# Reordered engine queues inside an attention slot, earlier operand splits, a third raw weight buffer and a ring of six accumulator banks

## The chip, the cores and the metric

One core of a Trainium2 chip runs the whole program. The metric is device time in microseconds (us), median of several runs. The engines of the core each work through a queue of their own in order: PE (matmul), ACT (activations and copies), DVE (vector work), POOL (a second, slower vector engine), and SP, which here only starts DMAs. They wait for each other through semaphores.

## The reference, cut to what matters

Causal attention by blocks of 64 over 4 batches, 8 heads and 576 positions of 64 values, followed by two feed-forward layers of 512 to 2048 to 512 over the 2304 tokens.

```python
def _attn_ref(q, k, v):
    scores = scale * np.matmul(q, k.transpose(0, 1, 3, 2))
    mask = block_i >= block_j
    scores = np.where(mask, scores, -1000000000.0)
    scores = scores - np.max(scores, axis=-1, keepdims=True)
    attn = np.exp(scores)
    attn = attn / (np.sum(attn, axis=-1, keepdims=True) + 1e-09)
    return np.matmul(attn, v)

def _moe_ref(x, w_in, w_out, alpha):
    h = x @ w_in
    g = np.maximum(h, 0.0) + alpha * np.minimum(h, 0.0)
    return g @ w_out

def _moe2_ref(x, w_in, w_out):
    h = x @ w_in
    g = np.where(h > 0.0, h, np.exp(np.minimum(h, 0.0)) - 1.0)
    return g @ w_out
```

The weights arrive as 64-bit floats; the kernel turns each into two 32-bit parts itself.

## The kernel before, in words

**Three passes for one product.** Every operand of a matmul is split into a high and a low part (`fp32r`), and a product is three matmuls: high by high, high by low, low by high (`PASSES`). So q, k, x, the gates and the weights all need a "high" copy and then a "low" one, which is the value less its high part. `copy("p", ...)` (line 88) puts a high part on POOL, `low_part` (line 81) a low part on DVE or POOL, `q_low` (line 226) the low part of q on DVE.

**Attention in slots.** `SEQ` lists 64 slots. The first 16, called early here, take one pair of heads each over the first 256 positions. The other 48, called late, go three to a pair of heads: i = 2 and i = 3 take 128 queries each, i = 4 the last 64 of both heads. `slot(k)` (line 459) writes one slot into the queues, and the order of its lines is the order on every engine: `scores` (PE), the product with v of an older slot (`second`, PE), the transposes of a slot two or three back (PE), then the sums and reciprocals of the slot before (`normalise`, DVE, and the scaling of p on POOL, line 88), then `maxima` (memsets of the mask and the maxima, DVE), the gates that wait in `held`, the copies of the finished x (`out`, ACT then DVE), the copies of the transposes (`move`, ACT and DVE), then `exponentials` (ACT, line 321), and at the end whatever was planned for the slot in `other_at`. Scores go to one of two PSUM pairs in turn, transposes to banks 4 and 5, x to banks 6 and 7.

**Splits and loads.** `load_early` and `load_late` start the DMAs of the raw q and k, `split_early_k`, `split_early_q`, `split_k` and `split_late_q` make the parts. Early slots share one split for two slots (a duo d, used in slots 2d and 2d+1). The plan is in lines 441 to 453: k of a duo at the end of slot 2d-2, q at the end of slot 2d-1; in the late part k three slots ahead and q two slots ahead of the first use.

**Weights.** `load_w` (line 110) starts one DMA of 512 KB into a buffer `wraw` (pool of two), and plans five steps for the following ticks: two on ACT, three on DVE (lines 130, 131, 135), one on POOL (line 140), a cast on ACT and the low part on DVE.

**The first layer beside the attention.** `l1_beside` puts the matmuls of the first layer for three token units between the slots from slot 11 on (lines 527 and 550).

**After the attention** only the order on PE is written by hand. Steps go over token units (five of 512, 512, 512, 512 and 256) and blocks of 128 hidden values: `l1_h` or `l2_h` makes one bank of h (lines 527, 571), and two steps later `l1_y` or `l2_y` adds its product into four accumulator banks (lines 614, 589). h goes round a ring of four banks, the accumulators are banks 2 to 5 for every unit (`ACC`). At a unit's end the accumulators are copied out (`to_z`, line 531, or line 621).

Of the kernel before, what the change touches and what calls it, by code (L numbers as in the profile page):

```python
# [19 lines left out]
P = 128  # L20
# [21 lines left out]
def attention_moe_kernel(ctx: ExitStack, tc: tile.TileContext, qT, kT, v_a, v_b, w1, w2, alpha, out):  # L42
# [6 lines left out]
    wraw_p = ctx.enter_context(pool("wraw", 2))  # L49
# [7 lines left out]
    nc.sync.dma_start(out=alpha_sb, in_=alpha)  # L57

    beta = const.tile([P, NF], F32, name="beta")
    dve.tensor_scalar(beta, alpha_sb, -1.0, 1.0, ALU.mult, ALU.add)  # L60
# [134 lines left out]
    def load_early(d):  # L195
        b, hs = duo(d)
        st[2 * d]["raw"] = raws = raw_tiles()
        for t, src in zip(raws[::-1], (kT, qT)):
            for a in range(2):
                h = slice(hs.start + 2 * a, hs.start + 2 * a + 2)  # L200
                nc.sync.dma_start(out=t[:, 256 * a:256 * a + 256],
                                  in_=src[b, h].rearrange("e p s -> (e p) s")[:, :256])
# [33 lines left out]
    def split_q(n, c):  # L236
        s = st[n]
        q = s["raw"][0]
        s["q"] = tiles = [ap2.tile([P, 512], F32R, tag=f"q{x}", name=f"q{x}") for x in "hl"]
        qh, ql = (t[:, :c.stop - c.start] for t in tiles)  # L240
        copy("a" if c.start == 0 and n == 0 else "p", qh, q[:, c], 0.125)
        q_low(ql, q[:, c], qh)
# [5 lines left out]
    def split_early_q(d):  # L248
        split_q(2 * d, slice(0, 512))
        st[2 * d + 1]["q"] = st[2 * d]["q"]  # L250

    def split_late_q(n):
        s = st[n]
        split_q(n, slice(256, 512))
        s["diag"] = dh, dl = qdiag[n % 2]
        q = s["raw"][0]
        for x in range(2):
            r, c = slice(64 * x, 64 * x + 64), slice(64 * x, 64 * x + 64)
            copy("p", dh[r, c], q[r, 512:], 0.125)
            q_low(dl[r, c], q[r, 512:], dh[r, c])  # L260
# [121 lines left out]
    def parts_of_x(n, half):  # L382
# [3 lines left out]
        if half == 1:  # L386
            tail = st[n]["tail"] = ap1.tile([P, 2, 64], F32R, tag="xtail", name="xtail")
            parts.append((slice(256, 320), lambda k: tail[:, k, :]))
# [12 lines left out]
    def second(n, half, chunks):  # L401
# [39 lines left out]
    for d in range(NP // 2):  # L441
        if d:
            plan(2 * d - 2, lambda d=d: split_early_k(d))
            plan(2 * d - 1, lambda d=d: split_early_q(d))
        if d > 1:
            plan(2 * d - 3, lambda d=d: load_early(d))
            plan(2 * d, lambda d=d: load_early_v(d))
    for n in range(NP):
        k = NP + 3 * n
        plan(k - 5, lambda n=n: load_late(n))  # L450
        plan(k - 3, lambda n=n: split_k(n, S))
        plan(k - 2, lambda n=n: split_late_q(n))
        plan(k + 2, lambda n=n: load_late_v(n))
    NORM = transposes_at.pop("norm")
# [4 lines left out]
    def slot(k):  # L459
# [15 lines left out]
        if here:  # L475
            exponentials(*here)
# [107 lines left out]

    def l2_y(u, f, gs):
        for tg in range(UNITS[u] // P):
            acc = bank[ACC[tg]]
# [17 lines left out]
    def l1_y(kind, u, f, gs):  # L605
# [5 lines left out]
        for m in range(KC):  # L611
            acc = bank[ACC[m]][:, :n]
# [14 lines left out]
    ACC = (2, 3, 4, 5)  # L627
    ET = mybir.EngineType
    with tc.manual_schedule(engines={ET.PE, ET.Activation, ET.DVE, ET.Pool, ET.SP}):
# [43 lines left out]
    with tc.manual_schedule(engines={ET.PE}):  # L673
# [7 lines left out]
        ring("h", 6, 7, 0, 1)  # L681
# [66 lines left out]
```

## Time and profile before

| what | value |
|---|---|
| median of 3 runs | 1078.89 us (1077.31 to 1943.81) |
| the profiled execution, its own time | 1077.87 us |
| span of the profiled execution | 1076.1 us |
| instructions | 13977 |
| mean granted clock of PE | 0.974 |
| PE busy | 989.7 us |

A row of the trace gives start and duration in us, engine, line, operation, and in brackets how long the engine was idle before it and what ended that. "PEclk" is the share of the full PE clock that was granted: 1.00 is 2.4 GHz, 0.50 is 1.2 GHz, and a value between them is a mix over the stretch.

### The profile page before, as it was taken

The numbers are of one execution on the slowest core, as the hardware profiler recorded it, in microseconds if no ns is written. First come the engines' busy times: TensorE is split into PE (matmuls) and PEld (weight loads), VectorE is DVE, ScalarE is ACT, GpSimd is POOL, SyncE is SP. The second block draws the span as 40 slices with busy tenths as digits, with TensorE's granted clock in tenths as the row PEclk, the third lists the DMA queues.
The fourth block names the chain that finished last, engine by engine and source line by source line (L and its number), as shares of the span: only waits on it lengthen the run. The fifth ranks groups of instructions, "written<-read, shape, count | busy, mean of one in ns | idle before, by whom it ended". The sixth has DMA issues, their size and how long they took to land.

```text
span 1076.1 us, 13977 instructions
## 1 busy us (share of the span) xinstructions
PE 989.7 (92%) x5072; PEld 789.9 (73%) x5072; DVE 560.8 (52%) x1067; ACT 440.5 (41%) x965; POOL 349.8 (33%) x410
## 2 busy tenths in 40 slices
PE   4667998988888999999999998899999999999998
PEld 3445765655557987788888886688888888888897
DVE  4677576776745787631131577873333333333343
ACT  4556565655544655432232455542222222222222
POOL 4665566765623555442232455420000000000000
PEclk9888998999899999999999999899999999999999
DMA  4461622452355655350230635510300300110010
GB/s 119 138 211 38 202 88 78 135 169 83 115 164 186 191 168 182 110 160 36 79 118 1 210 123 177 193 42 1 118 1 1 118 1 1 40 40 1 1 40 20
DMA packets 54437, 104.73 MB, mean 97 GB/s; under 512 B 10976, under 2 KB 28384, under 8 KB 53216
## 3 DMA queue, kind: packets, MB, share of 16 engines
q1 hardware_dynamic: 54368, 103.84, 29.7%
q8 instruction: 40, 0.66, 0.2%
q14 instruction: 29, 0.24, 0.1%
HBM read 75.51 MB, written 28.31 MB: 96 GB/s over the span
## 4 chain that ended last, share of the span: by engine, by line
PE 53%; DVE 15%; POOL 11%; DMA 7%; issue 6%; ACT 6%; SPq 1%; POOLq 0%; ACTq 0%
PE bank L589 17%; PE bank L571 16%; PE bank L614 7%; PE bank L527 7%; DMA wraw<-w 6%; POOL wword L140 3%; POOL p L88 3%; DVE wword L130 2%; DVE wword L135 2%; DVE wword L131 2%; ACT p L321 2%; DVE stat L293 2%; PE bank L550 2%; DVE w L81 2%; POOL gs L81 2%
## 5 line engine op out<-in xcount | busy, mean ns | idle before, releaser
L527 PE MATMUL bank<-x,w 128*128 128x512 f32 (+1 forms) x960 | 214.1, 372 | 3.6 <-DVE xtail L81 1.5
L571 PE MATMUL bank<-x,w 128*128 128x512 f32 (+1 forms) x960 | 211.2, 369 | 0.0
L527 PEld LDWEIGHTS bank<-x,w 128*128 128x128 f32 x960 | 169.2, 191 | 34.5 <-issue 1.6
L571 PEld LDWEIGHTS bank<-x,w 128*128 128x128 f32 x960 | 170.3, 189 | 31.6
L576 DVE TENSOR_SCALAR e<-e 128x512 f32<-128x512 f32 (+1 forms) x80 | 33.1, 414 | 169.2 <-ACT e L575 169.2
L575 ACT ACTIVATE e<-bank 128x512 f32<-128x512 f32 (+1 forms) x80 | 44.4, 555 | 181.8 <-PE bank L571 181.8
L140 POOL TENSOR_TENSOR wword<-wword,wraw 128x512 int32<-128x512 int32 x64 | 89.6, 1402 | 82.0 <-DVE wword L135 44.0
L589 PE MATMUL bank<-w,gsl 128*128 128x512 f32 x432 | 107.2, 395 | 3.8 <-DVE z L621 2.6
L510 DVE SCALAR_TENSOR_TENSOR g<-neg,beta,bank 128x512 f32<-128x512 f32 (+1 forms) x68 | 46.3, 681 | 116.1 <-ACT neg L507 116.1
L88 POOL TENSOR_SCALAR p<-p,stat 128x128 f32<-128x128 f32 (+4 forms) x144 | 79.7, 568 | 78.8 <-DVE stat L327 45.5
L589 PE MATMUL bank<-w,gs 128*128 128x512 f32 x432 | 104.9, 390 | 0.2 <-DVE gs L81 0.2
L614 PE MATMUL bank<-gsl,w 128*128 128x512 f32 (+1 forms) x408 | 90.9, 369 | 7.5 <-POOL gsl L81 3.0
L589 PEld LDWEIGHTS bank<-w,gsl 128*128 128x128 f32 x432 | 81.1, 190 | 22.1 <-ACT e L575 3.0
L81 POOL TENSOR_TENSOR gs<-g,gs 128x512 fp32r<-128x512 f32 (+1 forms) x46 | 57.7, 1254 | 111.9 <-ACT gs L514 103.6
L614 PE MATMUL bank<-gs,w 128*128 128x512 f32 (+1 forms) x408 | 89.5, 366 | 4.5 <-POOL gs L81 4.4
L589 PEld LDWEIGHTS bank<-w,gs 128*128 128x128 f32 x432 | 80.5, 188 | 17.0 <-DVE gs L81 0.7
L321 ACT ACTIVATE p<-pair,stat 128x128 f32<-128x128 f32 (+4 forms) x144 | 78.3, 552 | 34.9 <-DVE stat L293 32.9
L614 PEld LDWEIGHTS bank<-gsl,w 128*128 128x128 f32 x408 | 71.2, 191 | 22.1 <-POOL gsl L81 5.0
L614 PEld LDWEIGHTS bank<-gs,w 128*128 128x128 f32 x408 | 70.4, 189 | 18.8 <-POOL gs L81 6.1
L81 DVE TENSOR_TENSOR w<-wword,w 128x512 fp32r<-128x512 f32 x64 | 59.6, 934 | 25.0 <-ACT w L149 24.0
L507 ACT ACTIVATE neg<-bank 128x512 f32<-128x512 f32 (+1 forms) x68 | 36.9, 542 | 87.2 <-PE bank L527 87.1
L81 POOL TENSOR_TENSOR gsl<-g,gsl 128x512 fp32r<-128x512 f32 (+1 forms) x34 | 42.2, 1242 | 76.7 <-ACT gsl L514 71.9
(77 smaller groups left out, 1310.3 us busy)
## 6 DMA issues: line engine op xcount, KB each, us to landing
wraw<-w SPq DMA_DIRECT2D x64, 512.0 KB, 3.6
xd<-x SPq DMA_DIRECT2D x4, 2048.0 KB, 7.2
x<-xd SPq DMA_DIRECT2D x16, 512.0 KB, 7.7
x<-yd SPq DMA_DIRECT2D x4, 2048.0 KB, 8.6
vraw<-v_a SPq DMA_DIRECT2D x24, 256.0 KB, 2.9
kraw<-kT SPq DMA_DIRECT2D x16, 288.0 KB, 4.0
yd<-gsl SPq DMA_DIRECT2D x8, 512.0 KB, 4.7
yd<-gs SPq DMA_DIRECT2D x8, 512.0 KB, 6.2
```

Source lines behind the costliest of these rows:

```text
L81: return {"v": dve, "p": pool_e}[eng].tensor_tensor(out=out, in0=x, in1=f32(high), op=ALU.subtract)
L88: return pool_e.tensor_scalar(out, x, 1.0 if scale is None else scale, 1.0, ALU.mult, ALU.mult)
L140: pool_e.tensor_tensor(out=w, in0=w, in1=units, op=ALU.add)
L321: act.activation(out=out, in_=x, func=AF.Exp, bias=stat[:, k:k + 1], accum_out=stat[:, w + k:w + k + 1])
L507: act.activation(out=neg, in_=h, func=AF.Relu, scale=-1.0)
L510: dve.scalar_tensor_tensor(out=g, in0=neg, scalar=beta[:, f:f + 1], in1=h, op0=ALU.mult, op1=ALU.add)
L527: pe.matmul(h, w_in(0, f, wp_, kc), x[:, xp_, kc, :n], start=kc == 0 and t == 0, stop=kc == KC - 1 and t == 2)
L571: pe.matmul(h, w_in(1, f, wp_, kc), x[:, xp_, kc, :], start=kc == 0 and t == 0, stop=kc == KC - 1 and t == 2)
L575: act.activation(out=e, in_=h, func=AF.Exp)
L576: dve.tensor_scalar(e, e, 1.0, -1.0, ALU.min, ALU.add)
L589: pe.matmul(acc, gs[:, gp_, tg * P:(tg + 1) * P], w_out(1, f, wp_, 0, DM), start=f == 0 and t == 0, stop=f == NF - 1 and t == 2)
L614: pe.matmul(acc, w_out(0, f, wp_, m * P, P), gs[:, gp_, :n], start=first and t == 0, stop=last and t == 2)
```

## The change

1. In `slot`, `maxima` goes ahead of the sums (`NORM`), and `exponentials` directly behind them, ahead of the copies of x and of the transposes.
2. The splits come sooner. In the early part the high part of q and both parts of k at the end of slot 2d-3, the low part of q a slot later; in the late part the high parts of q move to three slots ahead, in front of k, and the low parts stay at two. Loads are started one to three slots sooner. The first loads are ordered anew, and the first q comes through ACT's queue.
3. `alpha` is loaded after the first weights; `beta` is first written by an ACT copy.
4. In `out` both ACT copies come ahead of both DVE low parts, and `xtail` has two buffers.
5. `wraw` and `wword` have three buffers; the tiles for gates outside `gp` go from four, used every second time, to two, used every third time.
6. After the attention h has a ring of two banks (6 and 7), and the accumulators go round a ring of six (0 to 5).

```diff
-    wraw_p = ctx.enter_context(pool("wraw", 2))
+    wraw_p = ctx.enter_context(pool("wraw", 3))
...
-    nc.sync.dma_start(out=alpha_sb, in_=alpha)
-
     beta = const.tile([P, NF], F32, name="beta")
-    dve.tensor_scalar(beta, alpha_sb, -1.0, 1.0, ALU.mult, ALU.add)
+    act.copy(beta, ident[:, :NF])
+
+    def load_alpha():
+        nc.sync.dma_start(out=alpha_sb, in_=alpha)
+        dve.tensor_scalar(beta, alpha_sb, -1.0, 1.0, ALU.mult, ALU.add)
...
-        for t, src in zip(raws[::-1], (kT, qT)):
+        for t, src, eng in zip(raws[::-1], (kT, qT), (nc.sync, nc.sync if d else nc.scalar)):
...
-    def split_q(n, c):
+    def split_q(n, c, low):
...
+        if low:
+            q_low(ql, q[:, c], qh)
+        else:
+            copy("a" if c.start == 0 and n == 0 else "p", qh, q[:, c], 0.125)
...
-            tail = st[n]["tail"] = ap1.tile([P, 2, 64], F32R, tag="xtail", name="xtail")
+            tail = st[n]["tail"] = ap2.tile([P, 2, 64], F32R, tag="xtail", name="xtail")
...
-                for c, dst in parts_of_x(n, half):
+                parts = parts_of_x(n, half)
+                for c, dst in parts:
                     act.copy(dst(0), op[:, c])
+                for c, dst in parts:
                     low_part("v", dst(1), op[:, c], dst(0))
...
-    for d in range(NP // 2):
-        if d:
-            plan(2 * d - 2, lambda d=d: split_early_k(d))
-            plan(2 * d - 1, lambda d=d: split_early_q(d))
+    for d in range(1, NP // 2):
+        plan(2 * d - 3, lambda d=d: split_early_q(d, False))
+        plan(2 * d - 3, lambda d=d: split_early_k(d))
+        plan(2 * d - 2, lambda d=d: split_early_q(d, True))
         if d > 1:
-            plan(2 * d - 3, lambda d=d: load_early(d))
+            plan(2 * d - 6, lambda d=d: load_early(d))
...
-        plan(k - 5, lambda n=n: load_late(n))
+        plan(k - 6, lambda n=n: load_late(n))
+        plan(k - 3, lambda n=n: split_late_q(n, False))
         plan(k - 3, lambda n=n: split_k(n, S))
-        plan(k - 2, lambda n=n: split_late_q(n))
+        plan(k - 2, lambda n=n: split_late_q(n, True))
...
+        if here:
+            maxima(*here)
         for emit in NORM.get(k, ()):
             emit()
         if here:
-            maxima(*here)
+            exponentials(*here)
         after = [h() for h in held]
         held.clear()
         for o in outs:
             o()
         if move:
             move()
-        if here:
-            exponentials(*here)
...
-        if late_pools and turn[0] % 2:
-            return late_pools[0].tile([P, 2, 512], F32R, tag="gsl", name="gsl", bufs=4)
+        if late_pools and turn[0] % 3 == 0:
+            return late_pools[0].tile([P, 2, 512], F32R, tag="gsl", name="gsl", bufs=2)
...
-            acc = bank[ACC[tg]]
+            acc = acc_bank(tg, f == 0)
...
-            acc = bank[ACC[m]][:, :n]
+            acc = acc_bank(m, first)[:, :n]
...
         load_early(0)
-        load_w(*halves.pop(0))
+        load_early(1)
+        split_early_q(0, False)
+        split_early_k(0)
+        split_early_q(0, True)
         load_early_v(0)
         load_w(*halves.pop(0))
-        load_early(1)
+        load_alpha()
+        for emit in other_at[-1]:
+            emit()
         load_early_v(1)
-        split_early_k(0)
-        split_early_q(0)
+        load_w(*halves.pop(0))
...
-        ring("h", 6, 7, 0, 1)
+        ring("h", 6, 7)
+        ring("acc", *range(6))
```

**DVE, two early slots.** The rows are those of DVE in slots 5 and 6, first as they stood. `stat` holds maxima, sums and reciprocals of a slot, `pair` its scores, `x` the finished attention output, `pt` the transposed p, `wword` a weight half in work.

```order
L326 TENSOR_SCALAR stat<-stat 128x4
L327 RECIPROCAL stat<-stat 128x4
L296 MEMSET pair_103 64x2x64 x2
L293 TENSOR_REDUCE stat<-pair_103 128x2 x2
L81 TENSOR_TENSOR x_310<-bank_106,x_310 128x256
L87 COPY pt<-bank_104 128x2x128
L226 SCALAR_TENSOR_TENSOR ql<-qraw,qh 128x512
L130 TENSOR_SCALAR wword<-wword 128x512
```

The same place on DVE in the changed kernel:

```order
L302 MEMSET pair_102 64x2x64 x2
L299 TENSOR_REDUCE stat<-pair_102 128x2 x2
L332 TENSOR_SCALAR stat<-stat 128x4
L333 RECIPROCAL stat<-stat 128x4
L83 TENSOR_TENSOR x_332<-bank_105,x_332 128x256
L89 COPY pt<-bank_103 128x2x128
L132 TENSOR_SCALAR wword<-wword 128x512
L133 TENSOR_SCALAR wword<-wword 128x512
L137 SCALAR_TENSOR_TENSOR wword<-wraw,wword 128x512
```

The maxima stand ahead of the sums of the slot before, and the low part of q has left this slot for the even one.

**ACT, an early slot.** The rows of ACT over slots 5 and 6 as they stood; `p` is the exponentials.

```order
L418 CAST x_310<-bank_106 128x256
L85 COPY pt<-bank_105 128x2x256
L321 ACTIVATE p_426,stat<-pair_103,stat 128x128 x2
L321 ACTIVATE p_426,stat<-pair_103,stat 128x256 x2
L418 CAST x_310<-bank_107 128x256
```

The same place on ACT in the changed kernel:

```order
L327 ACTIVATE p_439,stat<-pair_102,stat 128x128 x2
L327 ACTIVATE p_439,stat<-pair_102,stat 128x256 x2
L425 CAST x_332<-bank_105 128x256
L87 COPY pt<-bank_104 128x2x256
L327 ACTIVATE p_492,stat<-pair_101,stat 128x128 x2
```

The high part of x, on which DVE's low part of x waits, has gone from ahead of the slot's exponentials to behind them.

**POOL, a late pair of heads.** The rows of POOL as they stood, from the scaling of an i = 4 slot on; `gs` is a gate of the first layer, `kh` and `kl` the parts of k, `qh` and `qdiag` those of q.

```order
L88 TENSOR_SCALAR p_1607<-p_1607,stat 128x576
L81 TENSOR_TENSOR gs<-g,gs 128x512
L88 TENSOR_SCALAR kh<-kraw 128x576
L81 TENSOR_TENSOR kl<-kraw,kh 128x576
L88 TENSOR_SCALAR p_1654<-p_1654,stat 128x384 x2
L88 TENSOR_SCALAR qh<-qraw 128x256
L88 TENSOR_SCALAR qdiag_118<-qraw 64x64 x2
```

The same place on POOL in the changed kernel:

```order
L90 TENSOR_SCALAR p_1600<-p_1600,stat 128x576
L83 TENSOR_TENSOR gs<-g,gs 128x512
L90 TENSOR_SCALAR qh<-qraw 128x256
L90 TENSOR_SCALAR qdiag_117<-qraw 64x64 x2
L90 TENSOR_SCALAR kh<-kraw 128x576
L83 TENSOR_TENSOR kl<-kraw,kh 128x576
L90 TENSOR_SCALAR p_1652<-p_1652,stat 128x384 x2
```

The high parts of q have moved ahead of k and of the next scaling; their low parts on DVE stay where they were, one slot later.

## Rows read from the trace of the kernel before

**Rows 1.** The page, part 1: busy us, share of span, instructions per engine.
```profile
PE 989.7 (92%) x5072; PEld 789.9 (73%) x5072; DVE 560.8 (52%) x1067; ACT 440.5 (41%) x965; POOL 349.8 (33%) x410
```

**Rows 2.** Windows: stretch, length, busy per engine, then PEclk, DMA share, GB/s.
```profile
8.40:67.20 58.80, 39.21 (x264) 28.56 (x264) 39.84 (x107) 34.34 (x121) 36.94 (x62) 0.91 0.41 130
67.20:105.90 38.70, 26.29 (x167) 19.65 (x166) 28.22 (x62) 22.13 (x68) 21.23 (x35) 0.82 0.34 113
105.90:296.60 190.70, 170.76 (x1055) 116.15 (x1054) 132.85 (x331) 110.55 (x280) 120.31 (x172) 0.95 0.40 124
320.40:460.00 139.60, 130.04 (x731) 112.85 (x732) 94.97 (x137) 73.17 (x142) 69.27 (x57) 0.99 0.53 169
600.00:720.00 120.00, 112.19 (x473) 89.63 (x472) 97.43 (x138) 65.28 (x113) 54.21 (x37) 0.97 0.44 149
720.00:1020.00 300.00, 300.00 (x1325) 248.50 (x1324) 104.31 (x174) 70.88 (x117) 0.00 (x0) 1.00 0.08 29
```

**Rows 3.** Waits, whole program: waiter, what ended it, total us, times, longest.
```profile
ACT e L575 <- PE bank L571: 181.8, 71, 3.0
...
DVE ql L226 <- POOL qh L88: 34.2, 18, 4.3
ACT xtail L418 <- DVE x L81: 34.0, 14, 5.1
...
PE pair L276 <- POOL qh L88: 23.4, 6, 5.5
```

**Rows 4.** Timeline of the start, ACT and PE.
```profile
6.33 1.28 ACT L85 ACT_TABLE_LOAD   x1 [6.33 <-DMA qraw<-qT]
...
8.40 0.47 PE L276 MATMUL pair<-kh,qh 64*128 64x128 f32 x2 [8.40 <-ACT qh L85]
```

**Rows 5.** Timeline of one early slot from its maxima on, DVE and ACT.
```profile
46.81 0.42 DVE L296 MEMSET pair<- 64x128 f32 x2
...
48.20 0.41 DVE L81 TENSOR_TENSOR x<-bank,x 128x256 fp32r<-128x256 f32 x1
48.32 0.37 ACT L321 ACTIVATE p<-pair,stat 128x128 f32<-128x128 f32 x1 [0.70 <-DVE stat L293]
48.53 0.41 DVE L87 COPY pt<-bank 128x256 f32<-128x256 f32 x1
...
49.20 0.69 DVE L226 SCALAR_TENSOR_TENSOR ql<-qraw,qh 128x512 fp32r<-128x512 f32 x1 [0.26 <-POOL qh L88]
49.81 0.42 DVE L130 TENSOR_SCALAR wword<-wword 128x512 f32<-128x512 f32 x1
49.92 0.63 ACT L149 CAST w<-wword 128x512 fp32r<-128x512 f32 x1
...
51.34 0.16 DVE L326 TENSOR_SCALAR stat<-stat 128x4 f32<-128x4 f32 x1
...
51.73 0.42 DVE L296 MEMSET pair<- 64x128 f32 x2
```

**Rows 6.** Timeline, DVE: where the maxima of slots 4, 11 and 16 begin.
```profile
31.20 0.42 DVE L296 MEMSET pair<- 64x128 f32 x2 [1.09 <-PE pair L276]
...
69.32 0.42 DVE L296 MEMSET pair<- 64x128 f32 x2
...
106.80 0.17 DVE L301 MEMSET pair<- 64x128 f32 x1 [0.54 <-PE pair L276]
```

**Rows 7.** Late part: one timeline row of DVE, one wait of window 105.9:296.6.
```profile
254.68 0.44 DVE L226 SCALAR_TENSOR_TENSOR ql<-qraw,qh 128x256 fp32r<-128x256 f32 x1 [4.35 <-POOL qh L88]
...
PE bank L356 <- ACT pt L85: 12.7, 8, 2.5
```

**Rows 8.** Timeline, PE: first matmul into an accumulator bank at two unit changes.
```profile
349.63 0.63 PE L614 MATMUL bank<-gsl,w 128*128 128x256 f32 x3 [2.88 <-ACT z L85]
...
680.08 0.94 PE L589 MATMUL bank<-w,gsl 128*128 128x512 f32 x3 [2.57 <-DVE z L621]
```

**Rows 9.** Timeline, DVE and POOL: a low part of q beside POOL's addition.
```profile
74.96 1.27 POOL L140 TENSOR_TENSOR wword<-wword,wraw 128x512 int32<-128x512 int32 x1
75.03 1.75 DVE L226 SCALAR_TENSOR_TENSOR ql<-qraw,qh 128x512 fp32r<-128x512 f32 x1 [2.73 <-POOL qh L88]
```

More of the change, by code (lines that the diff above doesn't have):

```diff
@@ L197, in load_early @@
         st[2 * d]["raw"] = raws = raw_tiles()
-        for t, src in zip(raws[::-1], (kT, qT)):
+        for t, src, eng in zip(raws[::-1], (kT, qT), (nc.sync, nc.sync if d else nc.scalar)):
             for a in range(2):
                 h = slice(hs.start + 2 * a, hs.start + 2 * a + 2)
-                nc.sync.dma_start(out=t[:, 256 * a:256 * a + 256],
-                                  in_=src[b, h].rearrange("e p s -> (e p) s")[:, :256])
+                eng.dma_start(out=t[:, 256 * a:256 * a + 256], in_=src[b, h].rearrange("e p s -> (e p) s")[:, :256])
     def load_early_v(d):
@@ L234, in split_k @@
         low_part("v" if width == 512 and n == 0 else "p", kl, k, kh)
-    def split_q(n, c):
+    def split_q(n, c, low):
         s = st[n]
         q = s["raw"][0]
[L239 to L242, printed above, removed]
+        if not low:
+            s["q"] = [ap2.tile([P, 512], F32R, tag=f"q{x}", name=f"q{x}") for x in "hl"]
+        qh, ql = (t[:, :c.stop - c.start] for t in s["q"])
+        if low:
+            q_low(ql, q[:, c], qh)
+        else:
+            copy("a" if c.start == 0 and n == 0 else "p", qh, q[:, c], 0.125)
     def split_early_k(d):
@@ L246, in split_early_k, with split_early_q, split_late_q @@
         st[2 * d + 1]["k"] = st[2 * d]["k"]
-    def split_early_q(d):
-        split_q(2 * d, slice(0, 512))
+    def split_early_q(d, low):
+        split_q(2 * d, slice(0, 512), low)
         st[2 * d + 1]["q"] = st[2 * d]["q"]
-    def split_late_q(n):
+    def split_late_q(n, low):
         s = st[n]
-        split_q(n, slice(256, 512))
+        split_q(n, slice(256, 512), low)
         s["diag"] = dh, dl = qdiag[n % 2]
@@ L258, in split_late_q @@
             r, c = slice(64 * x, 64 * x + 64), slice(64 * x, 64 * x + 64)
-            copy("p", dh[r, c], q[r, 512:], 0.125)
-            q_low(dl[r, c], q[r, 512:], dh[r, c])
+            if low:
+                q_low(dl[r, c], q[r, 512:], dh[r, c])
+            else:
+                copy("p", dh[r, c], q[r, 512:], 0.125)
     EARLY_TILES = ((0, 0, 128), (1, 128, 384))
@@ L449, in attention_moe_kernel @@
         k = NP + 3 * n
-        plan(k - 5, lambda n=n: load_late(n))
+        plan(k - 6, lambda n=n: load_late(n))
+        plan(k - 3, lambda n=n: split_late_q(n, False))
         plan(k - 3, lambda n=n: split_k(n, S))
-        plan(k - 2, lambda n=n: split_late_q(n))
+        plan(k - 2, lambda n=n: split_late_q(n, True))
         plan(k + 2, lambda n=n: load_late_v(n))
+    for k in sorted(k for k in other_at if k < 0):
+        other_at.setdefault(-1, []).extend(other_at.pop(k)) if k < -1 else None
     NORM = transposes_at.pop("norm")
@@ L583, in l2_h, with acc_bank @@
         return gs
+    accs = {}
+    def acc_bank(m, first):
+        if first:
+            accs[m] = bank[take("acc")]
+        return accs[m]
     def l2_y(u, f, gs):
         for tg in range(UNITS[u] // P):
-            acc = bank[ACC[tg]]
+            acc = acc_bank(tg, f == 0)
             for t, (wp_, gp_) in enumerate(PASSES):
@@ L624, in l1_y @@
                 nc.sync.dma_start(out=yd[u][:, :, m, :], in_=f32(ys))
-    ACC = (2, 3, 4, 5)
     ET = mybir.EngineType
```

## The prediction

> **What bounds the kernel now.** I read the engine totals first, then the stretches, then the waits, then the timeline of one slot. PE is busy for 989.7 of 1076.1 us [rows 1], so all that can be won is the idle time of PE and the time in which it runs at the lower clock. The stretches show where these lie [rows 2]. From 720 to 1020 us PE is busy for all 300 us at a granted clock of 1.00: nothing to win. The slots from 8.40 to 105.90 us leave PE idle for (58.80-39.21) + (38.70-26.29) = 32 us, at a clock of 0.91 and 0.82. The late slots, 105.90 to 296.60, leave 20 us idle at 0.95. From 320 to 460 it is 9.6 us and from 600 to 720 it is 7.8 us. So the slots decide, and after them the two stretches with weights.
>
> In the slots no engine is full: DVE, the busiest beside PE, has 39.84 of 58.80 us [rows 2]. It is a chain of waits. Three of them stand out in the list [rows 3]: PE waits for POOL's high part of q (23.4 us, six times, up to 5.5), DVE waits for the same thing (34.2 us), and ACT waits for DVE between the two copies out of one bank (34.0 us).
>
> **The early slots, the loop that is left.** The splits that PE waits for go up to two slots ahead, so these waits should go. What is late next? I take one slot on DVE [rows 5]. From the memsets to the end of the maxima, that is to the next instruction, it takes 48.20-46.81 = 1.39 us. ACT starts the exponentials 0.12 us later and is through with them at 49.92, 1.60 us on. Today DVE meanwhile does the low part of x (0.33 to the next start), the copy of the transposes (0.41), the low part of q (0.61) and the three weight steps (51.34-49.81 = 1.53); then come the sums, 0.39 us, and the next slot's maxima: 51.73-46.81 = 4.92 us, with DVE hardly idle.
>
> In the new order the sums hide behind the exponentials, a gain of 0.39 us. But ACT's copy of x now stands behind the exponentials, and DVE's low part of x waits for it. So from the end of the maxima DVE waits 0.12 + 1.60 + about 0.38 for the copy (of the same shape as DVE's 0.41) + 0.05 = 2.15 us, and only then does it do the rest: 1.39 + 2.15 + 0.33 + 0.41 = 4.28 us and the extras behind it. In an even slot these are q's low part (0.61), 4.89 us; in an odd one the weight steps, 5.81 us; and a weight's low part, about 0.65, comes in slot 4 twice and in slots 8 and 10 once. Slots 4 to 10 sum to 4x4.89 + 3x5.81 + 4x0.65 = 39.6 us. Today they take 69.32-31.20 = 38.1 us [rows 6]. This part of the edit thus costs 1.5 us where one expects a gain: the wait for q is gone, and a wait for x has come in its place.
>
> Slots 11 to 15 take 106.80-69.32 = 37.5 us today [rows 6], 7.5 each, since PE has a first-layer piece of some 3 us in each slot, at half clock for a good part (granted 0.82 [rows 2]), and it stands still until q is split. In the new order the piece runs ahead of the scores and the gate hides in DVE's wait; DVE's loop gives 5.8 and less, PE at the full clock about 5.5. I take 6.0 each, 30 us: 7.5 less.
>
> **The start.** PE starts at 8.40 us, behind q's DMA, a table load of 1.28 us and the high part [rows 4]. The new order starts q's DMA beside k's and takes the table load out of the way, worth 3 us for PE. But the subtraction for `beta` now stands on DVE ahead of the first maxima and waits for a DMA behind 1.8 MB of others, so I give the first maxima 1.5 us only. Up to the maxima of slot 4 (31.20 today, where DVE had waited for scores that had waited for q): maxima 0 at 8.8, exponentials, both weight pieces on ACT (2.2 us) and their steps on DVE bring maxima 2 to 15.7; slot 2 has no x, 1.39+0.39+0.41+0.61 = 2.8; slot 3 is 4.28: maxima 4 at 22.8, or 8.4 us sooner. The DMAs must deliver 3 MB for that in 13 us, so I take 6. With slots 4 to 15: -6 + 1.5 - 7.5 = **-12 us** at the first late slot. Bounds: without any loss from x it would be -22; with DVE slowed as under the third rival, +7.
>
> **The late slots.** 15 pairs of heads take 190.7 us, 12.7 each [rows 2]. There the chain goes through POOL: gate, both parts of k, scaling of p, then q, and DVE stands idle for q, as in the row with 4.35 us [rows 7]; behind it come the low part of x, ACT's second copy, the copy of the transposes and at last PE (12.7 us of waits for that copy [rows 7]). The edit puts q's high part ahead of k and a slot ahead of its low part, and takes ACT's wait out of the copies of x. Left are two loops. PE has 170.8 us of work, of which (1-0.95) x 2 x 190.7 = 19 us of the stretch ran at 1.2 GHz and would shrink by some 8.5: 162 us, 10.8 a pair. DVE has 132.85/15 = 8.9 us a pair and now waits in the slot of i = 4 for exponentials and two copies, about 1.4: 10.3. Both loops are close together and hold each other up, so I don't take 10.8 but 11.5, nearer to the lower bound than to today's 12.7 because the three named waits, not the work, fill the gap: 15 x 1.2 = **-18 us**. Bounds: -28 (10.8 a pair) and 0.
>
> **After the attention.** At a unit's change PE waits for the copy of the accumulators: 2.88 and 2.57 us in the two rows [rows 8], with five smaller ones behind them about 8 us. Six banks let two of the four sums start on free ones; the other two come 0.7 us of matmul later each, so I take 7. The third raw buffer: SP may start a weight's DMA one piece sooner; I give it 1, between 0 and 3. Two h banks in place of four: the next-but-one h must wait for the gate of the first, which has three pieces of 2.7 us, 8 us, to be read in. In the second layer ACT has nothing else to do and sits waiting for PE for 181.8 us [rows 3]; nothing there. In the stretches with weights a late gate holds PE up anyway through the product; I cost it at nothing and bound it by +5. The gate tiles come round after six in place of eight and are needed for three or four: nothing. **-8 us**, between -11 and +4.
>
> **Sum.** 1077.87 - 12 - 18 - 8 = 1039.9, say 1040 us, from the profiled execution, which is 1.0 us under the median of the runs shown. A measurement of this kernel can tell about 2% from no change, 21.6 us; faster begins at 1057.
>
> **A rule against this change.** In the rows, a low part of q beside POOL's addition took 1.75 us [rows 9] and one with POOL idle 0.69 [rows 5]. The Trainium skill, page "SBUF — State Buffer", section "Who interferes with whom", says that a DVE instruction with two SBUF inputs contends with a GpSimd (POOL) instruction that reads SBUF. The two rows agree with it. By that rule denser slots would give part of their gain back on DVE, which is the third rival.
>
> **Rivals.**
> First, PE becomes dense: 10.8 us a pair, the early slots lose nothing to x (-18), and -10 after the attention: 1078 - 28 - 18 - 10 = 1022 us. For it speaks that in the new order nothing on POOL is late; against it the loop of 4.28 us and more. Chance 0.17.
>
> Second, the late slots stay where they are, because ACT's copies of the transposes now stand behind the exponentials and PE's next transposes wait for them as they do now: 1078 - 12 - 8 = 1058 us. For it: 12.7 us of PE's waits are for that very copy [rows 7]. Against: the copy is late today because ACT waits for DVE, and the exponentials are over some 4 us after the scores, when PE still has its x and a first-layer piece to do. Chance 0.16.
>
> Third, slower: DVE's loop grows under POOL's reads. With q's low part at 1.75 (+1.06) and each weight step stretched in the same measure (+2.2 in an odd slot) slots 4 to 10 take 50 us, 12 more than today, slots 11 to 15 gain nothing, and a late pair takes 10.3 + 1.1 + 1.3 = 12.7, no gain: 1078 - 6 + 12 - 8 = 1076 at an unchanged clock. If with these gaps the late clock falls from 0.95 to the 0.82 of the stretch before, 0.26 of 190.7 us more run at 1.2 GHz, some 25 us: about 1100 us. It decides from 12.7 us a pair on. For it are the rows of 1.75 us; against it that POOL has the same work as before, so that the mean shouldn't change. Chance 0.10.
>
> That the change doesn't do what it says is no case here: the queues show the new order.
>
> **How the numbers follow.** The forecast gets 0.57, with 1028 to 1055 as its own range. The range of 1016 to 1076 takes in the first two rivals and leaves out most of the third and the tails of the first, some 0.17. Faster: the forecast but for 0.02, the first rival, and a little of the second, 0.75. Same: most of the second and a part of the third, 0.17. Slower: 0.08.
>
> **What would show it.** Right: no wait of PE for POOL's q; DVE's low part of x waits for ACT about 2 us in each early slot; maxima of slots 4 to 10 some 5.6 us apart; the first late slot near 94 us; late pairs near 11.5 us; after the attention no waits on accumulator copies. Wrong: late pairs above 12.5 us, waits of PE for ACT's copies or of h for a gate, or DVE's q rows near 1.7 us throughout.

## The result and the profile after

The changed kernel takes 1089.84 us (median of five runs, 1087.34 to 1091.87) against 1078.89 before: ratio 1.0108 with a 95% interval of 1.0084 to 1.0132. It is slower by about 1%; forecast were 1040 us. One of the five runs of the kernel before took 1943.81 us, the others 1077 to 1079, and the ratio leaves it out. The profiled execution took 1091.87 us with a span of 1090.1, 14.0 us more than the profiled one before.

The engine totals, which answer to [rows 1]:

```profile
PE 992.5 (91%) x5072; PEld 792.7 (73%) x5072; DVE 595.4 (55%) x1067; ACT 439.8 (40%) x966; POOL 365.2 (34%) x410
```

PE, DVE and POOL run as many instructions as before, and yet DVE is busy for 35 us more and POOL for 15. The stretches of the changed kernel, with the columns of [rows 2]; the first holds slots 4 to 10, the second the late slots:

```profile
25.49:75.56 50.07, 33.78 (x196) 24.64 (x198) 32.79 (x76) 24.05 (x83) 25.62 (x45) 0.69 0.39 122
...
105.20:298.40 193.20, 166.99 (x1049) 116.39 (x1048) 156.82 (x336) 114.32 (x290) 126.74 (x175) 0.96 0.40 127
320.40:460.00 139.60, 125.72 (x717) 109.18 (x718) 95.74 (x139) 72.76 (x144) 74.43 (x56) 1.00 0.51 169
600.00:735.00 135.00, 118.21 (x493) 91.84 (x492) 107.80 (x138) 66.00 (x113) 54.01 (x37) 0.99 0.36 128
735.00:1035.00 300.00, 300.00 (x1329) 248.55 (x1328) 103.90 (x172) 70.35 (x116) 0.00 (x0) 1.00 0.08 29
```

In the late slots DVE is busy for 157 of 193 us, in place of 133 of 191. In the stretches with weights PE stands still for 14 and 17 us, in place of 10 and 8. The dense stretch behind them is as before. The maxima of slots 4, 11 and 16 on DVE, which answer to [rows 6], and three from the end of the late slots:

```profile
25.49 0.42 DVE L302 MEMSET pair<- 64x128 f32 x2 [0.62 <-PE pair L282]
...
75.56 0.42 DVE L302 MEMSET pair<- 64x128 f32 x2 [3.19 <-PE pair L282]
...
106.93 0.17 DVE L307 MEMSET pair<- 64x128 f32 x1
...
280.39 0.17 DVE L307 MEMSET pair<- 64x128 f32 x1
...
289.58 0.17 DVE L307 MEMSET pair<- 64x128 f32 x1
...
302.69 0.17 DVE L307 MEMSET pair<- 64x128 f32 x1
```

The same three in the kernel before:

```profile
284.31 0.17 DVE L301 MEMSET pair<- 64x128 f32 x1
...
289.97 0.17 DVE L301 MEMSET pair<- 64x128 f32 x1
...
302.30 0.17 DVE L301 MEMSET pair<- 64x128 f32 x1
```

Against [rows 6] the start gained 5.7 us, slots 4 to 10 lost 12.0 (50.07 in place of 38.12), and slots 11 to 15 gained 6.1 (31.37 in place of 37.48). The late slots changed by 0.3: their last maxima with a mask begin at 302.69 in place of 302.30. The other 13.6 us were lost behind these, nearly all of it after the attention. The sum is the 14.0 us of the two profiles.

The waits say what took the place of the old ones. The first three are of the whole program, the last three of PE alone from 322 to 735 us (waiter, what ended the wait, total us, times, longest):

```profile
POOL p L90 <- DVE stat L333: 81.2, 44, 7.8
...
DVE x L83 <- ACT x L425: 22.3, 16, 1.8
...
DVE x L83 <- ACT xtail L425: 17.1, 15, 2.7
...
PE bank L538 <- DVE g L521: 10.6, 7, 2.1
PE bank L632 <- POOL gs L83: 7.1, 9, 2.7
PE bank L582 <- DVE e L588: 4.6, 3, 2.3
```

PE's waits for POOL's `qh` [rows 3] are gone from the list, as intended. In their place DVE waits 39 us for ACT's copies of x, and after the attention PE waits for gates.

### The profile page after: what moved, and what is told of

The parts are those of the page before. It is cut to its first block, busy times and chain, and to the rows that moved or that the text cites. A ratio compares the mean times of both kernels' runs of the same rounds, so it can differ in the third digit from the quotient of the medians.

```text
span 1090.1 us, 14028 instructions
## 1 busy us (share of the span) xinstructions
PE 992.5 (91%) x5072; PEld 792.7 (73%) x5072; DVE 595.4 (55%) x1067; ACT 439.8 (40%) x966; POOL 365.2 (34%) x410
## 4 chain that ended last, share of the span: by engine, by line
PE 61%; DVE 21%; ACT 6%; DMA 4%; POOL 4%; issue 3%; SPq 0%; POOLq 0%; ACTq 0%; DVEq 0%
PE bank L607 18%; PE bank L582 17%; PE bank L538 10%; PE bank L632 9%; DVE wword L137 4%; DVE w L83 4%; DVE wword L133 3%; DVE stat L299 3%; ACT p L327 3%; DMA wraw<-w 3%; DVE wword L132 2%; PE bank L561 2%; PE bank L418 2%; POOL p L90 1%; PE bank L362 1%
## 5 line engine op out<-in xcount | busy, mean ns | idle before, releaser
L538 PE MATMUL bank<-x,w 128*128 128x512 f32 (+1 forms) x960 | 218.2, 377 | 15.7 <-DVE g L521 10.6
L607 PE MATMUL bank<-w,gs 128*128 128x512 f32 x588 | 143.1, 390 | 1.5 <-DVE zl L639 0.9
L607 PEld LDWEIGHTS bank<-w,gs 128*128 128x128 f32 x588 | 109.4, 188 | 24.9 <-DVE zl L639 1.3
L632 PE MATMUL bank<-gs,w 128*128 128x512 f32 (+1 forms) x540 | 119.1, 366 | 7.8 <-POOL gs L83 7.1
L632 PEld LDWEIGHTS bank<-gs,w 128*128 128x128 f32 x540 | 93.3, 188 | 27.2 <-POOL gs L83 10.2
L83 POOL TENSOR_TENSOR gs<-g,gs 128x512 fp32r<-128x512 f32 (+1 forms) x57 | 72.4, 1270 | 116.0 <-ACT gs L525 114.8
L418 PE MATMUL bank<-pt,vraw 128*64 128x320 f32 (+3 forms) x448 | 62.6, 404 | 20.0 <-DVE pt L89 10.2
L607 PE MATMUL bank<-w,gsl 128*128 128x512 f32 x276 | 66.9, 389 | 0.0
L418 PEld LDWEIGHTS bank<-pt,vraw 128*64 128x64 f32 (+1 forms) x448 | 29.9, 149 | 49.0 <-ACT pt L87 22.0
L299 DVE TENSOR_REDUCE stat<-pair 128x2 f32<-128x256 f32 (+3 forms) x80 | 63.3, 808 | 3.1 <-PE pair L288 1.2
L632 PE MATMUL bank<-gsl,w 128*128 128x512 f32 (+1 forms) x276 | 61.4, 368 | 2.0 <-POOL gsl L83 1.4
```

The source lines that it names most:

```text
L83: return {"v": dve, "p": pool_e}[eng].tensor_tensor(out=out, in0=x, in1=f32(high), op=ALU.subtract)
L299: peak = lambda out, x, axis=AX.X: dve.tensor_reduce(out=out, in_=x, axis=axis, op=ALU.max, negate=True)
L418: pe.matmul(op[64 * x:64 * x + 64, lo:qn], s["v"][:rows, x, j, :], s["pt"][:rows, x, o + lo:o + qn], start=j == 0, stop=j == nch - 1, skip ...
L538: pe.matmul(h, w_in(0, f, wp_, kc), x[:, xp_, kc, :n], start=kc == 0 and t == 0, stop=kc == KC - 1 and t == 2)
L607: pe.matmul(acc, gs[:, gp_, tg * P:(tg + 1) * P], w_out(1, f, wp_, 0, DM), start=f == 0 and t == 0, stop=f == NF - 1 and t == 2)
L632: pe.matmul(acc, w_out(0, f, wp_, m * P, P), gs[:, gp_, :n], start=first and t == 0, stop=last and t == 2)
```

## The experiments

Three theories stood at first. A: the new banks cost the time (two banks for h, a ring of six for sums). B: the third raw buffer costs it. C: the order within a slot costs it. Each run has the kernel before on the same chip beside it; ratios are to that.

| kernel | us | ratio to before, 95% interval |
|---|---|---|
| changed kernel | 1089.84 | 1.0108 [1.0084, 1.0132] |
| e1 old banks | 1086.67 | 1.0092 [1.0068, 1.0116] |
| e2 two raw buffers | 1073.71 | 0.9966 [0.9952, 0.9979] |
| e3 old slot order | 1063.77 | 0.9878 [0.9854, 0.9902] |
| e7 old slot order, old banks | 1060.34 | 0.9844 [0.9824, 0.9863] |
| e5 maxima first, exponentials last | 1061.70 | 0.9858 [0.9840, 0.9876] |
| e6 sums first, exponentials early | 1096.58 | 1.0186 [1.0166, 1.0206] |
| e8 old slot order, two raw | 1049.49 | 0.9739 [0.9720, 0.9757] |
| e9 the same, old banks | 1047.50 | 0.9725 [0.9708, 0.9743] |
| f1 copies of x before the exponentials | 1070.37 | 0.9923 [0.9903, 0.9943] |
| f2 copies of the transposes before them | 1082.67 | 1.0038 [1.0022, 1.0054] |
| f4 three raw, two working buffers | 1071.88 | 0.9944 [0.9927, 0.9960] |
| f3 best: order of e5, two raw, old banks | 1043.66 | 0.9688 [0.9670, 0.9706] |
| f6 before, exponentials early | 1110.88 | 1.0301 [1.0277, 1.0325] |
| f5 before, third buffer | 1093.02 | 1.0133 [1.0116, 1.0150] |
| f7 best, larger gate pool | 1049.01 | 0.9738 [0.9710, 0.9765] |

**Which part costs: e1, e2, e3, e7.** Each undoes one part of the changed kernel, the last one two.

```diff
-        ring("h", 6, 7)
-        ring("acc", *range(6))
+        ring("h", 6, 7, 0, 1)
...
-            accs[m] = bank[take("acc")]
+            accs[m] = bank[2 + m]
```

> The changed kernel with four banks for h and four fixed accumulator banks again; all else as changed. Theory A (two h banks make PE wait for gates after the attention; in the trace of the changed kernel twelve gaps of 1.1 to 2.3 us stand between 355 and 706 us, 18 us in all): these waits go, and the accumulator waits of before (about 8 us) come back, so about 1080 us, 8 to 12 below the changed kernel's 1089.8. Theory B (the third raw buffer bunches the weight steps on DVE, and any bank plan would wait): 1087 to 1092.

1086.67 us: 3 us less, with an interval that overlaps that of the changed kernel. A falls as the main cause. With four banks for h PE waits no longer for gates that free a bank (10.6 + 4.6 + 3.0 us in the changed kernel); from 322 to 735 us it waits for POOL's low parts of the gates in their place, 17.4 us. The gates are late under either bank plan:

```profile
PE bank L632 <- POOL gs L83: 12.8, 9, 3.4
PE bank L632 <- POOL gsl L83: 4.6, 3, 2.1
```

```diff
-    wraw_p = ctx.enter_context(pool("wraw", 3))
+    wraw_p = ctx.enter_context(pool("wraw", 2))
```

> The changed kernel with two buffers for raw weights and for words again; all else as changed. Theory A: the gates are late in a stretch where DVE has two weight halves per step in any case, so the PE waits for gates stay: 1086 to 1093. Theory B (the third buffer bunches the steps): the waits of h for gates fall by more than half, about 1080 us.

1073.71 us: 16 us less from this one number. B holds, and is larger than expected.

```diff
+        for emit in NORM.get(k, ()):
+            emit()
         if here:
             maxima(*here)
-        for emit in NORM.get(k, ()):
-            emit()
-        if here:
-            exponentials(*here)
...
         if move:
             move()
+        if here:
+            exponentials(*here)
```

> The changed kernel with the old order inside a slot (sums, maxima, copies, exponentials last); splits, loads, buffers and banks as changed. Theory C (the copies of x behind the exponentials cost DVE 1.8 us a slot, which eats what the earlier splits give): slots 4 to 10 fall from 6.6 to about 4.9 us each, the late slots to about 12 us a pair, 15 to 25 us in all: 1065 to 1075. Theory D (POOL's earlier splits slow DVE, whatever the order): the slots stay where they are, 1086 to 1093.

1063.77 us: 26 us less. C holds too. In the profiles the same matmul comes 5 us sooner at 57 us, 11 at 80, 26 by the end of the attention, and 26 to 29 from there: this cost lies in the slots.

> The old order inside a slot and the old banks together; left of the change are the earlier splits and loads, the order of the copies of x, the third raw buffer and the gate tiles. If A and C hold and are separate, the gains of e1 and e3 add: 1055 to 1068, below both kernels. If D holds, about 1080.

1060.34 us: 3.4 less than e3, again for the old banks.

**Which half of the order: e5, e6.** The order change has two halves, the maxima ahead of the sums and the exponentials ahead of the copies. e5 keeps the first alone, e6 the second. Between these I had two theories: N, the sums and with them POOL's scaling come late because they now wait behind maxima; X, the copies behind the exponentials hold up DVE.

```diff
         if here:
             maxima(*here)
         for emit in NORM.get(k, ()):
             emit()
-        if here:
-            exponentials(*here)
...
         if move:
             move()
+        if here:
+            exponentials(*here)
```

> The changed kernel with half of its new slot order: maxima still ahead of the sums, but the exponentials back at the end, behind the copies. Theory N (the sums of the slot before now wait behind maxima, which wait for PE's scores, so POOL's scaling of p and PE's transposes come late; POOL waits 40.7 us for the reciprocals between 106 and 287 us in the changed kernel, 11.0 with the whole old order): this stays slow, 1078 to 1092. Theory X (ACT's copies of x behind the exponentials hold up DVE): it comes back to the old order's time, 1062 to 1070, without waits of DVE's x for ACT.

1061.70 us. The whole cost of the order goes with the exponentials; maxima ahead of the sums is about 2 us better than the old order of e3, with overlapping intervals.

```diff
+        for emit in NORM.get(k, ()):
+            emit()
         if here:
             maxima(*here)
-        for emit in NORM.get(k, ()):
-            emit()
         if here:
             exponentials(*here)
```

> The other half: sums ahead of the maxima as in the kernel before, exponentials ahead of the copies as in the changed one. Theory N: 1062 to 1072, POOL's wait for reciprocals in the late part near 11 us though DVE's x still waits for ACT. Theory X: 1080 to 1092. Both parts at work: 1072 to 1080.

1096.58 us, though the sums stand first: above the range of X, and far from that of N. N falls and X holds. The long wait of POOL for the reciprocals, which had made N look strong, doesn't tell fast from slow: between 30 and 290 us it is 41.3 us in e5, the fastest of these, 41.9 in e6, the slowest, and 69.2 in the changed kernel.

**Which copies: f1, f2.** Both keep the exponentials ahead of one kind of copy only.

```diff
-        if here:
-            exponentials(*here)
         after = [h() for h in held]
         held.clear()
         for o in outs:
             o()
+        if here:
+            exponentials(*here)
         if move:
             move()
```

> The changed kernel with the copies of x ahead of the exponentials again; the copies of the transposes stay behind them. Theory X1 (DVE's low part of x waits for ACT's copy behind the exponentials, and DVE's copy of the transposes stands behind it): back to 1060 to 1070. Theory X2 (PE waits for ACT's own copies of the transposes, late behind the exponentials, 13 us of waits for a bank between 106 and 287 us in the changed kernel): stays at 1080 to 1092.

1070.37 us: 19.5 of the 28 us that lie between the changed kernel and e5.

```diff
         after = [h() for h in held]
         held.clear()
-        for o in outs:
-            o()
         if move:
             move()
+        if here:
+            exponentials(*here)
+        for o in outs:
+            o()
```

> The mirror of the run before: copies of the transposes ahead of the exponentials, copies of x behind them. X1 alone: 1080 to 1092. X2 alone: 1060 to 1070. Both matter: each of the two runs lands between, near 1075.

1082.67 us: 7 of the 28. The two shares add up to nearly all of it, and neither theory holds alone. Where each share lies is read from the maxima on DVE: slots 4 to 10 take 50.1 us in the changed kernel, 34.3 in f1, 48.0 in f2 and 36.1 in e5; a late pair of heads takes 12.6, 12.4, 12.15 and 11.9. In the early slots the copies of x decide; in the late ones each kind is worth a few tenths of a microsecond per pair, the transposes somewhat more.

**Why the third buffer costs: f4.** The pool holds two kinds of tile, the raw halves and the working buffers `wword`. f4 leaves three of the one and takes two of the other.

```diff
-            w = wraw_p.tile([P, DM], F32, tag="wword", name="wword")
+            w = wraw_p.tile([P, DM], F32, tag="wword", name="wword", bufs=2)
```

> The changed kernel with three raw buffers but two of the working buffers (wword). Theory R1 (with three halves in work at once DVE gets their steps in bunches ahead of gates that PE waits for): like two raw buffers, 1072 to 1076. Theory R2 (the third transfer starts sooner and collides with the others, or the smaller gate pool matters): 1086 to 1092.

1071.88 us, as with two of both. The third raw buffer by itself costs nothing; the third half in work does.

**The parts added up: e8, e9, f3, f7.** e8 puts the edits of e3 and e2 together, e9 those of e1 too, f3 is e5 with two raw buffers and the old banks, and f7 is f3 with the gate tiles of the kernel before (four, every second time).

> The changed kernel with the old slot order and two raw weight buffers; earlier splits, new start and bank rings stay. If the two costs add up (26 and 16 us below 1090): 1046 to 1050. If with the old slot order the third buffer is harmless: 1060 to 1065.

1049.49 us: the two costs add up to within 2 us.

> As the run before, with the old banks after the attention too (four for h, four fixed accumulators): only the earlier splits, the new start, xtail and the gate tiles of the change are left. If the six banks cost 3 us as with three raw buffers: 1043 to 1047. If the six banks gain once the weights keep up: 2 to 6 us above the run before, with PE's waits for accumulator copies of 2.5 to 2.9 us back.

1047.50 us, 2 less, within the measurement. In e8 PE waits 2.6 us for the gate that frees an h bank, 1.9 for POOL's low part of a gate and 1.5 for an accumulator's copy; in e9 the first is gone, and the others are 5.3 and 2.4 (PE from 310 to 715 us, first e8, then e9):

```profile
PE bank L538 <- DVE g L521: 2.6, 5, 0.7
...
PE bank L632 <- POOL gs L83: 1.9, 4, 0.7
...
PE bank L632 <- ACT z L87: 1.5, 1, 1.5
```

```profile
PE bank L632 <- POOL gs L83: 5.3, 6, 2.4
PE bank L632 <- ACT z L87: 2.4, 2, 1.9
```

One wait has been traded for others. What e9 keeps of the change (earlier splits and loads, the new start, the order of the copies of x with `xtail`, the gate tiles) is worth 2.75%; which of these brings how much was not tried.

> What has proved itself so far, in one kernel: maxima ahead of the sums, exponentials last, two raw buffers, the banks of the kernel before, with the change's earlier splits and start. If the gains add up (2 us from the maxima under 1047.5): 1043 to 1049, ratio about 0.971.

1043.66 us, ratio 0.9688: faster than both kernels by more than 3%. DVE is 15.5 us less busy than in the changed kernel (579.9 us), and a late pair takes 11.6 us.

```diff
-        if late_pools and turn[0] % 3 == 0:
-            return late_pools[0].tile([P, 2, 512], F32R, tag="gsl", name="gsl", bufs=2)
+        if late_pools and turn[0] % 2:
+            return late_pools[0].tile([P, 2, 512], F32R, tag="gsl", name="gsl", bufs=4)
```

> The best version so far (1043.7) with the larger gate pool of the kernel before. If the smaller gate pool costs nothing, as predicted: 1041 to 1046. If gates had to wait for tiles: 1035 to 1040.

1049.01 us: the larger gate pool is 5 us slower, neither of the two cases. The same matmuls run level until 330 us and fall behind at two places after the attention, 3 us by 355 (half of it made good later) and 4 more between 623 and 723; why was not tried.

**The two costs by themselves: f6, f5.** Is it the company of the other edits that makes them cost?

```diff
         if here:
             maxima(*here)
+        if here:
+            exponentials(*here)
...
-        if here:
-            exponentials(*here)
         for a in after:
```

> The kernel before with one move: the exponentials directly behind the maxima, ahead of the copies of x and of the transposes. If the move costs by itself: slower by 15 to 30 us, 1093 to 1108. If it costs only together with the earlier splits, because PE waits for POOL's q here anyway: within 6 us of 1078.

1110.88 us: 32 us lost by this one move in the kernel before. Between 30 and 330 us DVE's wait for x, 4.5 us before, has become 42.6, and PE's wait for the transposes, 14.4 us before, 25.8:

```profile
DVE x L81 <- ACT x L418: 42.6, 28, 2.1
...
PE bank L356 <- ACT pt L85: 25.8, 19, 2.6
```

f5 is the kernel before with the pool of three and the smaller gate pool, which makes room for it.

```diff
-    wraw_p = ctx.enter_context(pool("wraw", 2))
+    wraw_p = ctx.enter_context(pool("wraw", 3))
...
-        if late_pools and turn[0] % 2:
-            return late_pools[0].tile([P, 2, 512], F32R, tag="gsl", name="gsl", bufs=4)
+        if late_pools and turn[0] % 3 == 0:
+            return late_pools[0].tile([P, 2, 512], F32R, tag="gsl", name="gsl", bufs=2)
```

> The kernel before with three raw and three working weight buffers and the smaller gate pool that makes room for them. If the third buffer costs by itself: 1088 to 1096. If it costs only with the new banks or order: 1075 to 1081.

1093.02 us: 14 us lost. That the smaller gate pool is what costs here is unlikely, since in f3 it is the faster one. Both costs stand without the other edits.

## Why the prediction was wrong

**The start (-6): the number right, its reason only in part.** The maxima of slot 4 came 5.7 us sooner. PE started 3.4 us sooner (5.03 in place of 8.40), close to the 3 that were worked out, but the very first maxima came only 0.8 us sooner (9.59 in place of 10.35). In e3, which has the new loads and splits but the sums ahead of the maxima again, the maxima of slot 4 begin at 30.13, 1.1 us sooner than before; in e5, with the maxima first, at 25.20. So most of these 5.7 us hang on the place of the maxima, which the prediction doesn't name here.

**Slots 4 to 10 (+1.5): mis-sized, +12.0.** The wait that the prediction worked out is there to a few hundredths. One slot of the changed kernel, all engines:

```profile
57.70 0.42 DVE L302 MEMSET pair<- 64x128 f32 x2
...
60.88 0.38 ACT L425 CAST x<-bank 128x256 fp32r<-128x256 f32 x1
...
61.23 0.62 POOL L90 TENSOR_SCALAR qh<-qraw 128x512 fp32r<-128x512 f32 x1
61.29 0.42 DVE L83 TENSOR_TENSOR x<-bank,x 128x256 fp32r<-128x256 f32 x1 [1.82 <-ACT x L425]
...
61.63 0.41 DVE L89 COPY pt<-bank 128x256 f32<-128x256 f32 x1
...
61.96 0.75 DVE L132 TENSOR_SCALAR wword<-wword 128x512 f32<-128x512 f32 x1
62.19 1.55 PE L418 MATMUL bank<-pt,vraw 128*64 128x256 f32 x8 [1.45 <-DVE pt L89]
...
62.52 1.31 POOL L83 TENSOR_TENSOR kl<-kraw,kh 128x512 fp32r<-128x512 f32 x1
62.75 1.37 DVE L133 TENSOR_SCALAR wword<-wword 128x512 uint32<-128x512 uint32 x1
...
64.15 0.69 DVE L137 SCALAR_TENSOR_TENSOR wword<-wraw,wword 128x512 uint32<-128x512 uint32 x1
64.86 0.42 DVE L302 MEMSET pair<- 64x128 f32 x2
```

The maxima begin at 57.70 and x's low part at 61.29: 3.59 us, where 1.39 + 2.15 = 3.54 were worked out. DVE stands still for 1.82 of it. Behind it stands DVE's copy of the transposes, and behind that PE. The failed step is the next one: I took the three weight steps at 1.53 us, from a slot in which POOL let them run; here they take 64.86-61.96 = 2.90, and the slot 7.16 in place of 5.81. The three odd slots give 4.1 of the 10.5 us over the forecast, the even slots 4, 6 and 8 give 1.3, and slot 10 5.2 (10.7 us, of which DVE waited 3.19 for PE): a first-layer piece of twelve matmuls stands there ahead of the next scores, and it took 5.49 us (68.93 to 74.42), where one at 102.27 us took 3.00. PE's clock was granted at 0.69 in these slots, in place of 0.87, and PE was busy for 33.78 of the 50.07 us.

The sums hidden behind the exponentials, 0.39 us a slot, were booked as a gain. f1 shows what the place behind the exponentials cost: with x copied first, slots 4 to 10 take 34.3 us, less than before the change.

**Slots 11 to 15 (-7.5): nearly right, -6.1.** The full clock that was assumed for PE did not come: granted were 0.84 in this stretch (75.56 to 106.93), 0.82 before.

**The late slots (-18): failed, +0.3.** The step was "takes ACT's wait out of the copies of x. Left are two loops." The copies were put behind the exponentials by the same edit, and PE's wait for ACT's copies of the transposes (12.7 us [rows 7]) stayed, 13.3 us between 106 and 287 us. That is the second rival's mechanism, weighed at 0.16. It holds for these slots, but not alone: with the copies of the transposes ahead again (f2) a pair takes 12.15 us in place of 12.6, and with the exponentials behind both kinds of copy (e5) 11.9. The third buffer seems to have a share too. By the maxima at 280.39 the changed kernel was 3.9 us ahead of the one before (284.31). From there to the next ones it takes 9.19 us in place of 5.66, and DVE has steps of three weight halves there; before, and with two raw buffers (e2, 6.22 us), of two. The loop of 11.5 us that I forecast exists once the exponentials stand last: 11.7 us in e3, 11.9 in e5, 11.6 in f3.

**After the attention (-8): wrong in sign, +13.6.** The failed step is "SP may start a weight's DMA one piece sooner; I give it 1, between 0 and 3": a gain, with no bound on the other side. The step priced the raw buffer's transfer; what the pool's third buffer sets is how many halves DVE may have in work. DVE and PE in one period of the changed kernel:

```profile
648.00 0.41 DVE L132 TENSOR_SCALAR wword<-wword 128x512 f32<-128x512 f32 x1
...
648.79 0.74 DVE L521 SCALAR_TENSOR_TENSOR g<-neg,beta,bank 128x512 f32<-128x512 f32 x1
649.45 0.68 DVE L137 SCALAR_TENSOR_TENSOR wword<-wraw,wword 128x512 uint32<-128x512 uint32 x1
...
649.59 3.02 PE L538 MATMUL bank<-x,w 128*128 128x512 f32 x12 [1.52 <-DVE g L521]
...
650.37 1.31 POOL L142 TENSOR_TENSOR wword<-wword,wraw 128x512 int32<-128x512 int32 x1 [2.84 <-ACT gs L525]
650.51 1.46 DVE L133 TENSOR_SCALAR wword<-wword 128x512 uint32<-128x512 uint32 x1
...
652.00 1.66 DVE L137 SCALAR_TENSOR_TENSOR wword<-wraw,wword 128x512 uint32<-128x512 uint32 x1
...
653.58 2.40 DVE L83 TENSOR_TENSOR w<-wword,w 128x512 fp32r<-128x512 f32 x2
655.90 0.41 DVE L132 TENSOR_SCALAR wword<-wword 128x512 f32<-128x512 f32 x1
...
656.69 0.74 DVE L521 SCALAR_TENSOR_TENSOR g<-neg,beta,bank 128x512 f32<-128x512 f32 x1
...
657.49 3.02 PE L538 MATMUL bank<-x,w 128*128 128x512 f32 x12 [1.54 <-DVE g L521]
```

DVE is never idle here. Between one gate (648.79) and the next (656.69) it takes the steps of two halves, 7.9 us. PE meanwhile has two pieces of twelve matmuls, is through with them 6.4 us after it began (649.59), and then waits 1.54 us for the gate (at 657.49). Over the same matmuls DVE finishes 14 halves in the changed kernel (54 us, 611.4 to 665.4) and 11 with two raw buffers (46.4 us, 604.6 to 651.0); the first row is of the changed kernel, the second of e2 (columns: busy us, mean ns, then idle before them):

```profile
L83 DVE TENSOR_TENSOR w<-wword,w 128x512 fp32r<-128x512 f32 x14 | 16.4, 1209 | 2.4 <-ACT w L151 2.4
```

```profile
L83 DVE TENSOR_TENSOR w<-wword,w 128x512 fp32r<-128x512 f32 x11 | 11.1, 1017 | 6.7 <-ACT w L151 6.6
```

With the third buffer the weights run ahead of the matmuls that need them, in the queue of the engine that also makes the gates, and PE pays. The old pool had been a brake that kept them in step. f4 shows that the working buffers do it, f5 that but for the smaller gate pool no other edit is needed. Counted in DVE's rows, 59 of the 64 halves have their `L137` step (`L135` in f5) ahead of the first layer's last gate in every kernel with three working buffers, slow or fast in the slots, and 54 to 56 in every kernel with two. That this is worth 14 to 16 us is measured; that the steps' place ahead of the gates is the way it acts is read from these rows and this count, and no run moved the steps alone.

The banks were the other term (-7). The waits for accumulators' copies [rows 8] did go: no row of PE waiting for a copy `z` of over 1 us is left from 322 to 735 us. But PE now waits for gates that free one of two h banks, which I had costed at nothing with a bound of +5. Three pairs of runs (the changed kernel and e1, e3 and e7, e8 and e9) each put the new banks 2 to 3.4 us behind the old; their intervals overlap, so a gain of 7 is excluded and a small loss is likely. The gate tiles, also costed at nothing, are 5 us better in the smaller pool (f3 against f7); why stays open.

**The third rival (slower, 0.10): its numbers came out, its cause only in part.** It said 50 us for slots 4 to 10, 12.7 a late pair and no gain there; measured were 50.1 and 12.6. DVE's steps did grow beside POOL, against the argument that with the same work on POOL the mean shouldn't change: ql's mean in slots 4 to 10 was 0.69 us before. But ql grew as much where the time is won: here it is in slots 4 to 10 of the changed kernel, with x's low part, then in f1:

```profile
L227 DVE SCALAR_TENSOR_TENSOR ql<-qraw,qh 128x512 fp32r<-128x512 f32 x4 | 4.4, 1091 | 0.0
L83 DVE TENSOR_TENSOR x<-bank,x 128x256 fp32r<-128x256 f32 x7 | 3.0, 425 | 12.6 <-ACT x L425 12.6
```

```profile
L227 DVE SCALAR_TENSOR_TENSOR ql<-qraw,qh 128x512 fp32r<-128x512 f32 x4 | 4.3, 1088 | 0.0
...
L83 DVE TENSOR_TENSOR x<-bank,x 128x256 fp32r<-128x256 f32 x7 | 2.8, 398 | 0.0
```

The mean of ql is the same, 1.09 us, and DVE's total is 595.4 us in both kernels. The stretch is 15.8 us shorter: the 12.6 us in which DVE waits for x are gone, and so are 1.9 us of DVE's work (30.89 us in place of 32.79; the three weight steps alone take 7.1 in place of 10.0). Against the kernel before (28.88 us) DVE's work in these slots grew by 3.9 us, not by the 12 of this rival. Most of the length is the queue standing still. Of the signs of being wrong that the prediction lists, the late pairs, PE's waits for ACT's copies and h's wait for a gate came out, and q rows near 1.7 us throughout did not.

What was right of the forecast is the value of the earlier splits together with the new place of the maxima: with the exponentials last (e5) the first late maxima begin at 91.0 us (106.93 in the changed kernel), where the first late slot was forecast near 94, and f3 ends at 1043.66, near the 1040 that the whole edit was to give. That it is so near is partly luck: against the kernel before, f3 gains 15.5 us up to the first late maxima (91.26), 14.6 in the late slots (last maxima at 272.18) and 4.2 behind them, where 12, 18 and 8 were forecast, and it does without the new banks, which were to be worth 7.

## What to carry to other kernels

Before an instruction is moved forward in an in-order queue, list who on the other engines waits for what it passes: here 1.6 us of exponentials ahead of a copy of 0.38 us stopped DVE for 1.8 us in each of slots 4 to 10, and PE behind it in several of them. A buffer count is also a limit on how far one stream may run ahead of another; before raising it, see which queue gets the extra work early and whether the bounding engine waits for something behind it. And of a wait that is long in the list, like POOL's 81 us, ask for a fast and a slow kernel that both have it before taking it for a cause.

## What the runs showed of the hardware that was not expected

A DVE step with one SBUF input was stretched beside POOL as much as one with two. The second weight step, `L133`, takes 1.46 us where POOL's addition runs beside it (the row at 650.51) and 1.37 beside the low part of k (at 62.75); its mean in slots 4 to 10 was 0.43 before and 1.13 after. The low part of q, with two, took 0.69 and 1.75 [rows 5, rows 9]. An instruction that reads a PSUM bank wasn't: x's low part took 0.42 us at 61.29, with POOL's `qh` (61.23, 0.62 us) beside it. The prediction had a row of this for the low part of q alone, and took it over to the weight steps, in its third rival, without one. The Trainium skill, page "SBUF — State Buffer", section "Who interferes with whom", says that a `tensor_scalar` too can take the port pair that DVE shares with POOL, and that the one that comes second is then blocked for the whole instruction of the first. The rows agree: the step of 1.46 us ends 0.29 us after POOL's addition does (650.37 + 1.31 = 651.68).
